# A speech joint network on one core: the first convolution of batch 0 by direct taps and two triple tiles instead of pair filtering

## The chip, the cores and the metric

The kernel runs on 1 core of one Trainium2 chip. The metric is the device time of one execution in microseconds (us). Five engines of the core work side by side, each with its own queue of instructions: PE (TensorE) multiplies matrices, DVE (VectorE), ACT (ScalarE) and POOL (GpSimd) work on elements, and SP (SyncE) issues the transfers (DMAs). Matrix products are written to PSUM, eight banks of 512 fp32 columns.

## The reference

x is 2 x 4000 x 512 (bf16). Two convolutions over time of five taps and stride 2 (computed as stride 1 and then halved), each followed by GELU, reduce 4000 steps to 2000 (h) and then 1000 (f); a joint network then adds each of 1000 steps to each of 8 label vectors, takes tanh, and multiplies by w_o.

```
xp = pad(x, 2)                                   # B, T, D = 2, 4000, 512; K = 5
h = gelu(sum(xp[:, i:i+T] @ w1[i] for i in range(5)))[:, ::2]
hp = pad(h, 2)
f = gelu(sum(hp[:, i:i+2000] @ w2[i] for i in range(5)))[:, ::2]
j = tanh((f @ w_f)[:, :, None] + (g @ w_g)[:, None])      # 2, 1000, 8, 512
out = j @ w_o                                             # 2, 1000, 8, 512
```

## The kernel before, in words

Everything is held with the 512 channels on partitions: four blocks k of 128 input channels, four blocks m of 128 output channels. A product of one weight slice with one operand is four matmuls (one for each k) into one PSUM bank (`mm`, L471).

**Three ways to compute the first convolution.**
- Direct (`direct`, L835): one product for each tap, 5 products of n columns for n outputs.
- Pair filtering (`Tile_`, L673): 7 products for 2n outputs, with filtered inputs (`xf`, `shift`) and filtered weights (`w1sums`, `w1sum13`). `c1`, `c2` and `c3` are its stages; between them ACT copies a bank out, and DVE adds it to another.
- Triples (`Triple` and `Unit`, L714 and L763): 9 products for 3n outputs. Operands are made by DVE and ACT (`step`): "planes" are three copies scaled by 2 on ACT, with a subtraction on DVE each; then nine sums on DVE (t2, tm, sm, t1, s1, t0, s0, ti, si) and two shifted copies on ACT (prev, next). Weights come from `w1part`. A Unit is one m of a tile, with stages `s1` to `s5`: t2; tm and sm; t1 and s1; t0 and s0; ti and si. Behind `s1` and `s2` ACT copies the bank out, behind `s3` DVE makes two posts (a SCALAR_TENSOR_TENSOR and a TENSOR_TENSOR), and three outputs go through ACT as GELU.

Batch 0's 2000 outputs are three tiles before: 504 outputs (blocks m = 0, 1 direct, m = 2, 3 pair-filtered), 504 pair-filtered, and `trip[0]` of 332 triples. `trip[1]` and `trip[2]` are batch 1 with 334 triples each, `trip[3]` and `trip[4]` the second convolution of both batches. Then comes the joint stage.

**Loads** (all on SP, in written order). `load_xr` brings two blocks of 128 x 4 rows of x untransposed; PE transposes them (L560), ACT and DVE copy them from PSUM to `xs`. Then the five taps of w1 in the order 0, 2, 4, 1, 3 (`load_w1`, L518; from the second on each waits until the load three places earlier has landed). Then transposing DMAs: four of 256 rows for `xs` (`load_x`), six of 336 rows for `xp[1]`, the operand of `trip[0]` (`load_x6`, L508), one small `xe` of the last 16 rows, of which POOL copies a column into `xp[1]` (`load_end`, L529), and six for batch 1. The rest (`load_rest`, `load_late`) is issued by slot in the loop over units.

**Order of the work.** `Plan` is a planner in the kernel itself. Each operation has an engine, what it reads and writes, and an estimated cost. `schedule` (L160) runs a list schedule (`once`) up to `PASSES` times, between passes `learn` (L190) shifts due times and holds back operations where PE stops, and the best order is kept. From `pl.pin = False` (L849) on, PE, POOL and SP take the lowest index that is ready, ACT and DVE the earliest due time. Loads keep their written order. The loop at L995 writes the stages of the units and at fixed slots (`when`, `steps`) the making of later operands, loads and weights. The banks are one list of eight; a unit takes a bank A at `s1` and a bank B at `s3`, and gives them back after `s4` and `s5`.

PE first multiplies zeros (`warm_mm`, 7 and 1 more).

Of the kernel before, what the change touches and what calls it, by code (L numbers as in the profile page):

```python
# [68 lines left out]
class Plan:  # L69
# [4 lines left out]
    PASSES = 32  # L74
# [85 lines left out]
    def schedule(self, pred):  # L160
# [16 lines left out]
        hold, best = [0.0] * n, None  # L177
# [12 lines left out]
    def learn(self, pred, got, late, hold):  # L190
# [5 lines left out]
        t, found = 0.0, False  # L196
        for i in order["pe"]:
            if start[i] - t > 0.1 and start[i] > 6.0:
                j = i
                for _ in range(30):  # L200
                    done = [(end[q] + (self.HOP if w else 0.0), q) for q, w in pred[j].items()]
                    if not done:
                        break
                    q = max(done)[1]
                    if self.ops[q].dma:
                        break
                    e, p = place[q]
                    if e in ("act", "dve") and p and start[q] > ready[q] + 0.03:
                        b = order[e][p - 1]
                        if start[b] < ready[q] - 0.02 and first[b] > first[q]:  # L210
                            hold[b] = max(hold[b], ready[q] - 0.01)
                        late[q] -= 0.1
                        found = True
                    j = q
            t = end[i]
        return found
# [128 lines left out]
def bass_standalone__seq2seq_rnn_t_joint__speech_kernel(  # L345
# [25 lines left out]
    NA, NB = 252, 504  # L371
    NT3 = (T2 + 2) // 3
    NL = 332
# [6 lines left out]
    NWARM = 7  # L380
    TAPS = (0, 2, 4, 1, 3)

    with ExitStack() as es:
# [22 lines left out]
        xr = [Buf(nc, f"xr{i}", [4, NK, P], BF16, h_off + 16384 + i * 4096) for i in range(2)]  # L406
        assert hT[0].end <= h_off + 16384 and xr[1].end <= cur[0]
        c_off = cur[0]
        cs = [at(f"cs{i}", [NT], FP32) for i in range(2)]
        ty = [at(f"ty{i}", [2, 256], FP32) for i in range(3)]  # L410
        s_off = cur[0]
        ws = [at(f"ws{i}", [NK, P * (2 if i == 2 else 1)], FP32) for i in range(3)]
# [6 lines left out]
        w1_h = at("w1_h", [NK, D], BF16)  # L419
        xe = [at(f"xe{b}", [NK, 16], BF16) for b in range(B)]  # L420
        assert cur[0] <= 229368, cur[0]
        sd = [Buf(nc, f"sd{i}", [3, 336], FP32, o) for i, o in enumerate((c_off, c_off + 4096, s_off + 4096))]
        assert sd[1].end <= ty[2].end and sd[2].end <= ws[2].end
# [6 lines left out]
        row = [Buf(nc, f"row{b}", [6, NK, 336], BF16, xt_off + b * xt[0].bytes) for b in range(B)]  # L430
# [57 lines left out]
        for ph in (2, 3):  # L488
            memset(xs[0][ph, :, 15:16])
# [5 lines left out]
        def load_xr(rt):  # L495
            dst = xr[rt][:].map(lambda a: a.rearrange("p r k c -> p (r k c)"))
            src = x[0, 4 * P * rt:4 * P * (rt + 1), :].rearrange("(p r) c -> p (r c)", r=4)
            return pl.dma("sp", lambda e: e.dma_start(dst.ap, src), (), (dst,))

        def load_x(s, ph, lo, hi):  # L500

            b, half = s // 2, s % 2
            i0 = half * NB + lo - 16
            dst = xs[s % 3][ph, :, lo:hi]
            src = x[b, 4 * i0 + ph:4 * (i0 + hi - lo - 1) + ph + 1:4, :]
            pl.dma("sp", lambda e: e.dma_start_transpose(out=dst.ap, in_=src), (), (dst,), nbytes=(hi - lo) * 2 * D, rate=175e3)  # L506

        def load_x6(i, b, ph, j0, col):  # L508

            r0 = b * T + 6 * j0 + ph  # L510
            dst = xp[i][ph, :, col:col + 336]
            src = x.rearrange("b t d -> (b t) d")[r0:r0 + 6 * 335 + 1:6, :]
            pl.dma("sp", lambda e: e.dma_start_transpose(out=dst.ap, in_=src), (), (dst,), nbytes=336 * 2 * D, rate=175e3, slack=0.0 if i == 1 else 1.0)  # L513

        came = [load_xr(rt) for rt in range(2)]
# [7 lines left out]

        came.append(load_w1(TAPS[0]))
# [4 lines left out]
        def load_end(i, b):  # L529
            memset(xp[i][4:6, :, 336:340])  # L530
            memset(xp[i][0:4, :, 337:340])
            for ph in (4, 0, 2, 1, 3, 5):
                load_x6(i, b, ph, 330, 0)
            e16, d = xe[b][:], xp[i][0:4, :, 336:337]
            pl.dma("sp", lambda e: e.dma_start_transpose(out=e16.ap, in_=x[b, T - 16:T, :]), (), (e16,), nbytes=65536)
            v = xe[b][:, 12:16].map(lambda a: a.rearrange("p k (r o) -> p r k o", o=1))
            pl.op("pool", lambda e: e.tensor_copy(out=d.ap, in_=v.ap), (v,), (d,), 0.15)  # L537

        load_end(1, 0)
        for ph in (4, 0, 2, 1, 3, 5):  # L540
            load_x6(2, 1, ph, 0, 16)
# [9 lines left out]
        for pp in range(2):  # L551
            for rt in range(2):
                for r in range(2):
                    bk = 4 * rt + 2 * r if not pp else 2 * rt
                    lo = bk * 1024 + pp * r * 512
                    pv = View(psb[:, lo:lo + 512].rearrange("p (k c) -> p k c", k=NK), np.array([bk]), True)

                    def fn(e, rt=rt, pp=pp, r=r, pv=pv):
                        for k in range(NK):
                            ins = e.transpose(pv.ap[:, k, :], xr[rt].h[:, 2 * r + pp, k, :], ident.h[:, :])  # L560
                        return ins
                    pl.op("pe", fn, (xr[rt][:], ident[:]), (pv,), 0.22 if pp else 0.43)
                    if not pp and not rt and r:
                        warm_mm(NWARM, NWARM + 1)
                    o = xs[0][2 * r + pp, :, 16 + rt * P:16 + (rt + 1) * P]
                    if pp or r:
                        act(o, pv, ACT.Copy)
                    else:
                        pl.op("dve", lambda e, o=o, pv=pv: e.tensor_copy(out=o.ap, in_=pv.ap), (pv,), (o,), vec_cost(o, (pv,)))

        def shift(src, off, dst, c0, n, which):

            r, d, kind = {"a0": (2, -1, 0), "a3": (0, 1, 2), "b1": (3, -1, 3)}[which]
            act(dst[kind, :, c0:c0 + n], src[r, :, off + d:off + d + n], ACT.Copy)

        def xf(src, off, dst, c0, n, which, keep=False):


            ph = lambda r: src[r, :, off:off + n]
            o = lambda kind: dst[kind, :, c0:c0 + n]  # L580
            h = NT // 2
            if which == "a0" and keep:
                tt("dve", o(0), src[2, :, off - 1:off - 1 + n], ph(2), sub)
            elif which == "b3" and keep:
                tt("dve", dst[0, :, h:h + n], ph(3), ph(1), sub)
            elif which == "a2" and keep:
                tt("dve", dst[1, :, h:h + n], ph(2), ph(0), sub)
            elif which == "a0":
                tt("dve", o(0), o(0), ph(2), sub)
            elif which == "a3":  # L590
                tt("dve", o(2), o(2), ph(0), sub)
            elif which == "b1":
                tt("dve", o(3), o(3), ph(1), sub)
            elif which == "b3":
                tt("dve", ph(3), ph(3), ph(1), sub)
            elif which == "a1":
                tt("dve", o(1), ph(0), ph(2), add)
            elif which == "a2":
                tt("dve", ph(2), ph(2), ph(0), sub)

        def operand(src, off, dst, c0, n, which, k, keep=False):
            if keep and which in ("b3", "a2"):
                return dst[("b3", "a2").index(which), k, NT // 2:NT // 2 + n]
            if which in ("a0", "a1", "a3", "b1"):
                return dst[{"a0": 0, "a1": 1, "a3": 2, "b1": 3}[which], k, c0:c0 + n]
            r = {"b3": 3, "b2": 1, "a2": 2}[which]
            return src[r, k, off:off + n]
# [239 lines left out]
        for w in ("b1", "a3"):  # L847
            t0.shift(w)
# [436 lines left out]
```

## Time and profile before

| | us |
|---|---|
| median of 3 runs (256.37 to 257.28) | 256.41 |
| the profiled execution | 257.11 |
| its span, first to last instruction | 255.3 |
| idle PE in the span | 8.4 |
| first matmul of the direct taps / of the triple tile | 8.27 / 37.42 |

| stretch (us) | PE busy | DVE busy | ACT busy |
|---|---|---|---|
| 0.00 to 6.40 | 5.21 | 1.00 | 2.08 |
| 6.40 to 12.80 | 5.00 | 3.94 | 3.64 |
| 12.80 to 19.20 | 6.36 | 6.10 | 5.70 |
| 19.20 to 25.60 | 6.40 | 6.27 | 5.92 |
| 25.60 to 32.00 | 6.40 | 6.14 | 3.98 |
| 32.00 to 38.40 | 4.99 | 5.23 | 5.64 |
| 38.40 to 44.80 | 5.79 | 6.40 | 6.04 |
| 64 to 128 | 64.00 | 52.49 | 46.71 |
| 128 to 192 | 63.95 | 52.55 | 63.27 |

The profile is one execution. Times in it are microseconds from the span's start; busy time of an engine is the union of its instructions, and what lies between them is idle, put down to what ended it. A line number such as L475 is that of the helper that records the operation, so operations are told apart by their tiles: `acc<-xs,w_sb` is a matmul that writes PSUM from the weights `w_sb` and the operand `xs`. SPq is SP's queue while it issues a DMA.

### The profile page before, as it was taken

What the parts mean: (1) busy time and instruction counts of PE and PEld (TensorE: products, weight loads), DVE (VectorE), ACT (ScalarE), POOL (GpSimd) and SP (SyncE); (2) the same over time, 40 slices, a digit from 0 to 9 for tenths busy, and PEclk for the clock granted to TensorE, in tenths of its full rate; (3) what the DMA queues carried; (4) which work ended last, traced back from release to release, by engine and by line L of the source; (5) the groups of instructions that cost most, each with busy time, mean ns of one, the idle gap of its engine ahead of it and who ended that gap; (6) DMA issues with size and microseconds to landing.
All of it is one profiled execution on the core that took longest, in us unless ns stands there. A gap on an engine that the chain in (4) does not pass through costs nothing.

```text
span 255.3 us, 5286 instructions
## 1 busy us (share of the span) xinstructions
PE 246.9 (97%) x1922; PEld 185.3 (73%) x1928; DVE 209.2 (82%) x335; ACT 214.2 (84%) x352; POOL 102.7 (40%) x107
## 2 busy tenths in 40 slices
PE   8799979999999999999999999999999999999994
PEld 4689965666666666667557878877778877787882
DVE  1699989994999998197346889789899999999673
ACT  3589689959968857885499999999999999999862
POOL 1000000000000000000708899787796999998800
PEclk9999999999999999999999999999999999999999
DMA  6999999979100015000001322342235266545565
GB/s 243 295 197 193 143 167 186 155 157 357 48 0 3 0 47 202 1 1 3 0 0 52 115 85 83 110 140 83 87 124 174 74 195 205 174 149 187 174 198 185
DMA packets 54631, 31.88 MB, mean 125 GB/s; under 512 B 31518, under 2 KB 54350, under 8 KB 54606
## 3 DMA queue, kind: packets, MB, share of 16 engines
q1 hardware_dynamic: 54318, 31.36, 46.2%
q8 instruction: 15, 0.25, 0.4%
q10 hardware_dynamic: 288, 0.20, 0.2%
q14 instruction: 10, 0.08, 0.1%
HBM read 7.86 MB, written 16.38 MB: 95 GB/s over the span
## 4 chain that ended last, share of the span: by engine, by line
PE 82%; SPq 7%; DMA 5%; ACT 2%; issue 1%; DVE 0%; POOL 0%
PE acc L475 82%; SPq L513 4%; SPq L506 3%; DMA w_sb<-in_w_dram 2%; DMA xe<-in_x_dram 2%; DMA xr<-in_x_dram 1%; ACT row L467 1%; ACT xp L467 0%; ACT sd L467 0%; DVE xp L462 0%; ACT w_x L467 0%; ACT hT L467 0%; POOL xp L537 0%; ACT ost L467 0%; SPq L493 0%
## 5 line engine op out<-in xcount | busy, mean ns | idle before, releaser
L462 DVE TENSOR_TENSOR og<-acc,sn 128x512 bf16<-128x512 f32 x84 | 55.5, 682 | 9.7 <-PE acc L475 7.2
L467 ACT ACTIVATE jT<-feT,geT 128x1000 bf16<-128x1000 f32 (+6 forms) x56 | 52.6, 1025 | 0.5 <-DVE feT L904 0.4
L475 PE MATMUL acc<-tw,ss 128*128 128x256 f16 x336 | 46.3, 273 | 0.0
L1027 ACT ACTIVATE sn<-acc 128x512 f32<-128x512 f32 x55 | 36.5, 675 | 2.6 <-PE acc L475 1.7
L475 PEld LDWEIGHTS acc<-tw,ss 128*128 128x128 f16 x336 | 32.5, 98 | 7.7 <-ACT sn L1027 0.2
L475 PE MATMUL acc<-row,w_sb 128*128 128x334 bf16 (+1 forms) x192 | 35.0, 305 | 0.0
L1090 POOL TENSOR_TENSOR ss<-jT 128x512 f16<-128x512 bf16 x24 | 29.1, 1225 | 12.5 <-ACT jT L467 10.4
L475 PE MATMUL acc<-wo_sb,jT 128*128 128x256 bf16 (+1 forms) x187 | 31.5, 292 | 0.3
L467 ACT ACTIVATE jX<-feT,geT 128x1000 bf16<-128x1000 f32 (+4 forms) x28 | 26.9, 1028 | 0.0
L475 PEld LDWEIGHTS acc<-row,w_sb 128*128 128x128 bf16 x192 | 18.4, 97 | 8.3 <-DVE acc L637 0.2
L475 PEld LDWEIGHTS acc<-wo_sb,jT 128*128 128x128 bf16 x192 | 18.7, 98 | 6.1
L467 ACT ACTIVATE hT<-acc 128x334 bf16<-128x334 f32 (+2 forms) x32 | 15.1, 483 | 8.3 <-PE acc L475 8.3
L459 POOL MEMSET hT<- 128x8 bf16 (+2 forms) x6 | 0.7, 148 | 51.2 <-ACT hT L467 46.6
L637 DVE SCALAR_TENSOR_TENSOR acc<-acc,sd 128x334 f32<-128x334 f32 (+1 forms) x20 | 10.1, 507 | 13.6 <-PE acc L475 13.4
L1028 DVE COPY sn<-acc 128x512 f32<-128x512 f32 x29 | 19.7, 682 | 1.3 <-PE acc L475 1.0
L467 ACT ACTIVATE sd<-acc 128x334 f32<-128x334 f32 (+1 forms) x40 | 17.4, 450 | 3.0 <-PE acc L475 2.6
L1090 POOL TENSOR_TENSOR ss<-jT,ss 128x512 f16<-128x512 bf16 x16 | 18.8, 1176 | 1.1 <-DVE ss L1090 0.7
L475 PE MATMUL acc<-xp,w_x 128*128 128x334 bf16 (+1 forms) x96 | 16.7, 304 | 1.4 <-DVE xp L462 1.4
L475 PE MATMUL acc<-hT,w_t 128*128 128x334 bf16 x96 | 17.6, 305 | 0.0
L475 PE MATMUL acc<-xp,w_sb 128*128 128x334 bf16 (+1 forms) x96 | 17.5, 304 | 0.0
L475 PE MATMUL acc<-wo_sb,ss 128*128 128x256 bf16 x112 | 17.0, 273 | 0.0
L462 DVE TENSOR_TENSOR row<-row 128x1336 bf16<-128x1336 bf16 (+1 forms) x20 | 16.7, 843 | 0.0
(110 smaller groups left out, 529.7 us busy)
## 6 DMA issues: line engine op xcount, KB each, us to landing
out_dram<-og SPq DMA_DIRECT2D x98, 128.0 KB, 2.0
w_sb<-in_w_dram SPq DMA_DIRECT2D x10, 512.0 KB, 5.5
out_dram<-ost SPq DMA_DIRECT2D x10, 128.0 KB, 2.0
xr<-in_x_dram SPq DMA_DIRECT2D x2, 512.0 KB, 3.6
wf_sb<-in_w_f_dram SPq DMA_DIRECT2D x1, 512.0 KB, 3.8
wg_sb<-in_w_g_dram SPq DMA_DIRECT2D x1, 512.0 KB, 4.8
wo_sb<-in_w_o_dram SPq DMA_DIRECT2D x1, 512.0 KB, 5.6
xp<-in_x_dram SPq DMA_TRANSPOSE x18, 4.8
```

The lines of the kernel that those rows point to most:

```text
L459: pl.op("pool", lambda e: e.memset(v.ap, 0.0), (), (v,))
L462: pl.op(eng, lambda e: e.tensor_tensor(out=o.ap, in0=a.ap, in1=b.ap, op=op), (a, b), (o,), 0.02 + 2.14e-3 * o.ap.free_size() if eng == "po ...
L467: pl.op("act", lambda e: e.activation(o.ap, i.ap, func, scale=scale, bias=0.0 if bias is None else bias.ap), rd, (o,), o.ap.free_size() * ...
L475: ins = e.matmul(o.ap, lhsT=l.ap, rhs=r.ap, start=start and n == 0, stop=stop and n == len(pairs) - 1, skip_group_check=not check)
L506: pl.dma("sp", lambda e: e.dma_start_transpose(out=dst.ap, in_=src), (), (dst,), nbytes=(hi - lo) * 2 * D, rate=175e3)
L513: pl.dma("sp", lambda e: e.dma_start_transpose(out=dst.ap, in_=src), (), (dst,), nbytes=336 * 2 * D, rate=175e3, slack=0.0 if i == 1 else 1.0)
L637: pl.op(eng, lambda e: e.scalar_tensor_tensor(out=o.ap, in0=a.ap, scalar=f, in1=b.ap, op0=ALU.mult, op1=add), (a, b), (o,), vec_cost(o, (a ...
L1027: pl.flex({"act": (lambda e: e.activation(o.ap, v.ap, ACT.Copy), 0.05 + n * 0.833e-3), "dve": (lambda e: e.tensor_copy(out=o.ap, in_=v.ap) ...
L1028: "dve": (lambda e: e.tensor_copy(out=o.ap, in_=v.ap), 0.065 + n * 1.04e-3)}, (v,), (o,))
L1090: fn = lambda e, o=S[i], x=x, y=y, op=op: e.tensor_tensor(out=o.ap, in0=x.ap, in1=y.ap, op=op)
```

## The change

- The untransposed loads are four blocks, of 128, 128, 128 and 64 partitions with two rows each (`XR`); PE transposes them into `eo`, even and odd rows apart, which lies where w2 comes later. ACT copies the even rows, DVE the odd ones.
- 444 outputs are computed directly, all four m, tap by tap into banks 0, 2, 4 and 6. `Tile_`, `xf`, `shift`, `w1sums` and what belongs to them are gone.
- `trip` has one more tile in front: `trip[0]` of NF = 184 triples from the new buffer `xa` (six transposing loads of 192 rows), `trip[1]` of NL = 336 triples from `xp[1]`. In `xa` the operand sm has a plane of its own. There are six tiles and 24 units, and the slots of what follows move by four.
- `xe` of batch 0 and its column copy are gone; POOL clears columns of `xp[1]` instead, two of them after the planes 4 and 5 have landed.
- The loads of `xa` stand between those of w1: after the third tap planes 4 and 0, after the fourth tap plane 2, after the fifth planes 1, 3 and 5. Then come those of `xp[1]`.
- `w1part` makes all of the triples' weights, the doubled tap 1 included (before, `w1twice` doubled it in place).
- Two bank lists, even (A) and odd (B), until the joint stage.
- The planner makes up to 100 passes, starts each from the best so far, and cycles through several steps and places. Five warm-up matmuls instead of eight.

```diff
-    PASSES = 32
+    PASSES = 100
...
-        for _ in range(self.PASSES):
-            got = self.once(pred, succ, late, hold)
-            if best is None or got[0] < best[0] - 1e-9:
-                best = got
-            if not self.learn(pred, got, late, hold):
+        for _ in range(self.PASSES):
+            new = list(late), list(hold)
+            if not self.learn(pred, best, *new, tried):
                 break
+            got = self.once(pred, succ, *new)
+            if got[0] < best[0] + 1e-9:
+                tried = tried + 1 if got[0] > best[0] - 1e-9 else 0
+                best, (late, hold) = got, new
+            else:
+                tried += 1
...
+    ND, NF = 444, 184
+    NL = 2 * NT3 - ND // 3 - NF
...
-    NWARM = 7
+    NWARM = 5
...
+    XR = [P] * ((ND + 1) // P) + [32 * -(-((ND + 1) % P) // 32)]
...
+        eo = Buf(nc, "eo", [2, NK, EW], BF16, w2_sb.end - w2_sb.bytes)
+        xa = Buf(nc, "xa", [7, NK, 224], BF16, xs[0].end - xs[0].bytes)
...
         came.append(load_w1(TAPS[0]))
-        for i in TAPS[1:]:
+        for i in TAPS[1:3]:
             came.append(load_w1(i, came[-3]))
-        for ph in (2, 3, 1, 0):
-            load_x(0, ph, 272, 528)
...
+        load_a(4, 0)
+        came.append(load_w1(TAPS[3], came[-3]))
+        load_a(2)
+        came.append(load_w1(TAPS[4], came[-3]))
+        load_a(1, 3, 5)
...
+        for ph in (4, 0, 2, 1, 3, 5):
+            load_x6(xp[1], 0, ph, JL, 0, slack=0.3)
+            if ph > 3:
+                memset(xp[1][ph, :, 335:336])
...
-        load_end(1, 0)
...
         def w1part(m):
...
             stt("dve", u, w(4), 4.0, w(0))
             stt("dve", u, w(2), 2.0, u)
             act(w1_x[1, :, sl], u, ACT.Copy, scale=1.0 / 3.0)
+            tt("dve", t, w(0), w(4), add)
+            tt("dve", v, t, w(2), sub)
+            act(w1_x[0, :, sl], v, ACT.Copy, scale=1.0 / 3.0)
+            tt("dve", w1_t[2, :, sl], t, w(2), add)
             tt("dve", w1_x[2, :, sl], w(1), w(3), sub)
+            tt("dve", w1_t[1, :, sl], w(1), w(3), add)
+            act(w1_t[0, :, sl], w(1), ACT.Copy, scale=2.0)
...
         def direct(i):
-            for m in (0, 1):
-                for s in range(2):
-                    r, d = tap_at[i][s]
-                    mm(ps.cols((4 + 2 * m) * NT + NA * s, NA),
-                       [(w1_sb[i, k, m * P:(m + 1) * P], xs[0][r, k, 16 + d:16 + d + NA]) for k in range(NK)],
-                       i == TAPS[0] and s == 0, i == TAPS[-1], False)
+            for m in range(NK):
+                mm(ps.cols(2 * m * NT, ND),
+                   [(w1_sb[i, k, m * P:(m + 1) * P], eo[i % 2, k, 15 + i // 2:15 + i // 2 + ND]) for k in range(NK)],
+                   i == TAPS[0], i == TAPS[-1], False)
...
-        for w in ("planes",) + STEPS[2:]:
+        for w in ("planes", "t2", "tm", "sm", "t1", "s1", "prev", "next", "t0", "s0", "ti", "si"):
             trip[0].step(w)
...
+        when(0, lambda: trip[1].step("planes"))
+        for i in range(1, 4):
+            steps(i, 1, (0, 2, 4, 8)[i], (1, 4, 8, 13)[i])
...
-        nu = 17
+        nu = 21
```

More of the change, by code (lines that the diff above doesn't have):

```diff
@@ L188, in schedule, with learn @@
         return order
-    def learn(self, pred, got, late, hold):
+    def learn(self, pred, got, late, hold, tried):
         _, order, start, end, ready, _ = got
         place = {i: (e, p) for e, o in order.items() for p, i in enumerate(o)}
-        first = list(late)
[L196 to L216, printed above, removed]
+        gaps, t = [], 0.0
+        for i in order["pe"]:
+            if start[i] - t > 0.05 and start[i] > 6.0:
+                gaps.append(i)
+            t = end[i]
+        if not gaps:
+            return False
+        kind, which = divmod(tried, len(gaps) + 1)
+        step, wait = ((0.1, True), (0.5, False), (0.0, True), (2.0, True), (0.3, False), (1.0, True))[kind % 6]
+        first = list(late)
+        for i in gaps if which == len(gaps) else gaps[which:which + 1]:
+            j = i
+            for _ in range(30):
+                done = [(end[q] + (self.HOP if w else 0.0), q) for q, w in pred[j].items()]
+                if not done:
+                    break
+                q = max(done)[1]
+                if self.ops[q].dma:
+                    break
+                e, p = place[q]
+                if e in ("act", "dve") and p and start[q] > ready[q] + 0.03:
+                    b = order[e][p - 1]
+                    if wait and start[b] < ready[q] - 0.02 and first[b] > first[q]:
+                        hold[b] = max(hold[b], ready[q] - 0.01)
+                    late[q] -= step
+                j = q
+        return True
     def once(self, pred, succ, late, hold):
@@ L550, in bass_standalone__seq2seq_rnn_t_joint__speech_kernel @@
         psb = ps.h[:, :].bitcast(BF16)
[L551 to L569, printed above, removed]
@@ L601, in operand @@
[L601 to L607, printed above, removed]
-        def weight(which, k, m):
-            sl = slice(m * P, (m + 1) * P)
-            taps = {"a0": 0, "b1": 1, "b3": 3, "a3": 4}
-            if which in taps:
-                return w1_sb[taps[which], k, sl]
-            return w1_h[k, sl] if which == "a1" else w1_t[{"a2": 0, "b2": 1}[which], k, sl]
@@ L755, in product @@
                 w, p = self.w[which]
-                n = NT3 if start else self.n
+                n = self.n
                 mm(ps.cols(bank * NT, n),
@@ L779, in s1 @@
             def s1(self):
-                self.A = banks.pop(0)
+                self.A = even.pop(0)
                 self.t.product("t2", self.m, self.A, True)
@@ L800, in s4 @@
                 self.t.out(0, self.m, self.pa())
-                banks.append(self.A)
+                even.append(self.A)
             def s5(self):
@@ L885, in bank @@
         def bank():
-            banks.append(banks.pop(0))
-            return banks[-1] * NT
+            even.append(even.pop(0))
+            return even[-1] * NT
         def ge():
@@ L1016, in sem_of @@
             return sems[key]
-        free = banks
+        even += odd
+        odd = free = even
         H = NT // 2
```

269 lines of the change are left out of this document (84 added, 185 removed).

## The prediction

> **What bounds the kernel now.** I read the page first: the busy line, the slices, the chain by engine.
>
> ```profile
> PE 246.9 (97%) x1922; PEld 185.3 (73%) x1928; DVE 209.2 (82%) x335; ACT 214.2 (84%) x352; POOL 102.7 (40%) x107
> ...
> PE   8799979999999999999999999999999999999994
> ...
> DVE  1699989994999998197346889789899999999673
> ...
> PE 82%; SPq 7%; DMA 5%; ACT 2%; issue 1%; DVE 0%; POOL 0%
> ```
>
> PE (TensorE) is busy 246.9 of 255.3 us: 8.4 us are idle, and the slices put them at the front and in the last slice. So the change can gain only in the first 60 us, by less PE time or by fewer stops. The waits of PE, and then the chain in order of time, say what the stops are:
>
> ```profile
> PE acc L475 <- DVE xp L462: 1.4, 1, 1.4
> PE acc L475 <- DMA w_sb<-in_w_dram: 1.4, 1, 1.4
> PE acc L475 <- DVE zero L482: 1.2, 1, 1.2
> PE acc L475 <- ACT sd L467: 0.6, 1, 0.6
> ```
>
> ```profile
> 28.45 4.81 DMA xe<-in_x_dram
> ...
> 33.31 0.45 POOL xp L537
> ...
> 33.79 1.33 ACT row L467
> ```
>
> 1.4 + 1.4 + 1.2 + 0.6 = 4.6 us; the other 3.7 are the tail, which the change leaves alone. The 1.2 us (zero tile) stay too. The stop of 1.4 us on `xp` is the start of the triple tile: 28 us of loads queue on SP up to the small `xe` load, then POOL, ACT and DVE follow it. The timelines of PE and of DVE (start, length, what) give durations; landings of loads are the issue rows of the trace, start plus time to landing.
>
> ```profile
> 5.43 1.44 PE L560 MATMUL acc<-ident,xr 128*128 128x128 bf16 x12
> 8.27 1.03 PE L475 MATMUL acc<-xs,w_sb 128*128 128x252 bf16 x8 [1.40 <-DMA w_sb<-in_w_dram]
> 9.13 0.61 PE L560 MATMUL acc<-ident,xr 128*128 128x128 bf16 x8
> 9.58 1.46 PE L475 MATMUL acc<-xs,w_sb 128*128 128x252 bf16 x12
> ...
> 37.42 2.45 PE L475 MATMUL acc<-xp,w_x 128*128 128x334 bf16 x16 [1.41 <-DVE xp L462]
> ```
>
> ```profile
> 10.82 0.69 DVE L462 TENSOR_TENSOR ws<-w_sb 128x512 f32<-128x512 bf16 x1 [1.79 <-DMA w_sb<-in_w_dram]
> ...
> 33.55 0.43 DVE L462 TENSOR_TENSOR w_x<-w_sb 128x512 bf16<-128x512 bf16 x1
> 35.14 0.86 DVE L462 TENSOR_TENSOR row<-row,xp 128x1336 bf16<-128x1336 bf16 x1 [1.16 <-ACT row L467]
> ```
>
> A matmul's step is the distance between starts. Eight of 252 columns take 9.13 - 8.27 = 0.86, so 107.5 ns; eight of 128 columns take 9.58 - 9.13 = 0.45, so 56 ns. Both are columns / 2.4 + 2.5 ns; the triples' 332 columns step by 141 ns in the same timeline. DVE works without a gap worth the name from 10.82 to 34 us. It is the second bound of this stretch, close behind PE.
>
> **PE, before and after.** Before: 248 matmuls of 252 columns x 107.5 = 26.7; 12 late transposes x 56 = 0.7; the triple tile 144 x 141 = 20.3. From 8.27 that is 55.9, and with stops of 1.4, 0.3 (18.3 to 18.6) and 0.6 the triple tile ends at about 58.3 us. After: direct 4 m x 5 taps x 4 k = 80 matmuls of 444 columns at 187.5 = 15.0; tile F (184 triples) 144 at 79.2 = 11.4; tile L (336) 144 at 142.5 = 20.5. Sum 46.9 against 47.7 before: PE time gains 0.8, all else must come from stops.
>
> A step of 79 ns for 184 columns is read between the rows of 128 (56 ns) and 252 (107.5), and the 16 matmuls of 16 columns at 120.64 take 0.55 us in all, so no weight load holds a step up there. The Trainium skill, TensorE: Matmul & The Clock Gate, section Back-to-back issue gap, says otherwise: for streams of weight load and matmul about 81 ns at 128 columns and 131 at 512. By that, as an estimate, 184 columns step by 88 ns and F is 12.7 us instead of 11.4; our 56 ns at 128 columns, each with its own weight load, speaks against it.
>
> **Start of direct.** Loads before the first tap: 896 KB of rows instead of 1 MB. The two 512 KB loads of before landed at 3.93 and 5.18, 1.25 us apart; quarters of that size land at about 3.3, 3.9, 4.6, 4.9. Two warm-up matmuls fewer (5 end at 3.3) leave PE no gap before the first rows. The 32 transposes then run at the early 107 ns (1.44 us for 12 above), some 3 us, and end near 6.5, copies at 7.3. The first weight (8.03 before) comes after 0.1 MB less: 7.7. Direct runs 7.7 to 22.7; its banks (0, 2, 4, 6) are free. Later taps are wanted 3 us apart and landed 1.4 to 2.1 apart before, so they are covered, even with three short transposes queued in front.
>
> **Loads on SP.** Before, a 344 KB transpose landed every 1.75 us (22.27 to 29.47, four steps), one of 262 KB every 1.5. 192 KB should take 1.1. After the third weight at 10.5: two transposes 12.7, weight 14.2, transpose 15.3, weight 16.9, three transposes 20.2, then L's six, 22 to 31. The fourth and fifth weight now wait on SP for the first and second (7.7, some 9.2), with every later transpose queued behind them; SP reaches them at about 8 and 10, after the transposes, so the wait is short. Before, `xp` came at 22.3 to 33.0 and `xe` at 33.3. Removed: `xe` with its SP issue of 1.2 us and the POOL copy (0.4), so nothing of L waits for 33.3 any more. Added: POOL clears one column of planes 4 and 5 after their landing (0.12 us for 32 elements at 27.39); behind it on POOL stand only other clears, and plane 4, landed at 22, is wanted at 33. Batch 1's loads follow as before, some 2 us sooner, and have 20 us in hand.
>
> **DVE, the sum that I take to decide.** Steps from the DVE timeline: 512 f32 0.60, STT 0.61 to 0.72, 512 bf16 0.33, 1008 bf16 0.60, 1328 bf16 0.77; 744 elements then take 0.455. Work from the third tap's landing (10.8 before, 10.5 after: the sums need taps 0 and 4) to L's first operand t2:
> - gone: 9 filter sums x 0.60 = 5.4 (three more lay ahead of 10.8), 6 pair posts x 0.34 = 2.0, 4 scalings x 0.21 = 0.8, and some 15 us of weight sums that come back in another form;
> - weights: per m two STT 1.33, three f32 1.8, two bf16 0.66 = 3.8, x 4 = 15.2. The four doublings of `w1_sb[1]` go from ACT in L to ACT in `w1part`;
> - F's operands: 3 planes + 9 sums = 12 x 0.455 = 5.5; F's posts: 4 x (0.40 + 0.27) = 2.7;
> - L: one plane and t2, 2 x 0.77 = 1.5.
> Sum 24.9, from 10.5: 35.4; with 0.8 us of dependent pairs and waits (before, DVE lost 1.5 on the same way, 1.2 of them to `xe`) 36.2. Before it was 37.3. So the cover for what was removed is not there: DVE has as much to do as before, only the wait for `xe` falls away. PE without stops would end F at 7.7 + 15.0 + 11.4 = 34.1, so PE stops for some 2 us in F and at L's start: F's third and fourth unit (t2 wanted at 25.9 and 28.7) wait for `w1part` of m = 2 and 3, of which DVE has done two by 22.7 (12.2 us of work, 5 of it F's operands).
>
> **ACT**: weights 12 x 0.52, four GELUs 2.0, F's copies 5 x 0.72, F's evictions 20 x 0.27, L's copies 3 x 1.22: 21 us of the 28 from 8 to 36. It hides, if its order is good; before, its order cost the 0.57 at 41.2, and I keep 0.4 for that.
>
> **Rest.** L's 8 posts and 10 sums and the next tile's operands are as before (DVE was done with them at 58.4 and then idle for 3.4 us), shifted by as much as L. Two bank pools of four instead of one of eight cost nothing: a unit holds its banks for under three units. The further passes of the planner can gain only where PE stops: after 41.78 it stops for some 0.3 us in all before the tail; a worse order there costs at most some tenths.
>
> **Sum.** L starts at 36.2, 0.4 stop, 20.5: 57.1 against 58.3. That is 1.2 us less span: 254.1 instead of 255.3, and with the 1.8 around the span 255.9 for the profiled execution (257.11). The median of the runs shown, 256.41, is 0.7 below that execution; I apply the difference to it: 255.2.
>
> **Rivals.**
> 1. Stops nearly vanish: DVE's order puts weights first and L's first operands land in slack. 7.7 + 46.9 + 0.4 = 55.0, 3.3 less: 253.1. For it: loads come earlier and ACT is freer; against it: the DVE sum. With DVE half-way there 254.2. Chance 0.2. By the skill's step (above) its best would be 254.4.
> 2. Nothing gained: DVE or ACT order loses what `xe` gave, or the PE clock starts late. Before, PE took 5.4 us of work (1.2 to 6.6) at 107 ns per 128 columns and was fast at 9.13, after a gap of 1.4 us. Fewer warm-ups and waits between four row loads may leave direct at half speed for up to 5.4 us: 2.7 lost, F ends at 36.8, L at 58.1. Range 255.8 to 257.5. Chance 0.2.
> 3. Slower: the twelve transposes keep the queue longer than their size says. An issue took up to 2.86 us beside weights (the second `xs` load). L's t2 needs the ninth (six of F, three of L), from 10.5 with 3.1 us of weights between. At 2.15 us each it lands at 33 and begins to hold L; from 2.5 us each L starts after 38.7 and the run is over 0.5% slower; at 2.86 each L starts at 42.3, 6.1 later than forecast: 261. Against it: 1.1 to 1.75 per transpose in the rows. Chance 0.1.
> The forecast, 254.6 to 255.8, has 0.5.
>
> **Chances.** A measurement of this kernel tells about 0.5% (1.3 us) from no change, so 255.1 and 257.7 are the bounds. Half of the forecast and all of rival 1 lie below 255.1, with a little of rival 2: faster 0.48. Same 0.42, slower 0.10. The range leaves out the best of rival 1 and all of rival 3: 253.4 to 257.0.
>
> **What would show it.** Right: 184-column matmuls 79 ns apart; direct from 7.7 at 187 ns; L's first matmul near 36 after a wait for DVE; DVE full from 10.5 to 57; no `xe` ahead of L. Wrong: PE waits for DMA in F (rival 3), 370 ns steps in direct (rival 2), L before 35 (rival 1), or new PE stops after 60 us, which no step here prices.

## The result, and the profile after

Slower by about half a per cent: 258.57 us (median of 22 runs, 256.19 to 260.61) beside 256.76 for the kernel before on the same chips; ratio 1.0054, interval 1.0028 to 1.0079. Two later series of the unaltered changed kernel gave 1.0028 (1.0000 to 1.0055) and 1.0044 (1.0016 to 1.0072); over all three its median is 257.9 (46 runs). A ratio leaves out runs that lie more than 1.5% above the fastest of the same kernel. The profiled execution took 257.44 us, with a span of 255.6 (before: 257.11 and 255.3), so it is one of the faster ones and shows only 0.3 us of the loss.

The page after, the same rows ("..." marks lines left out, here and below):

```profile
PE 248.5 (97%) x1901; PEld 180.0 (70%) x1901; DVE 207.0 (81%) x338; ACT 211.9 (83%) x356; POOL 102.6 (40%) x107
...
PE   6999989999999999999999999999999999999994
...
DVE  1299999981999999198346889789899999989673
...
PE 81%; DVE 8%; DMA 4%; SPq 4%; issue 1%; ACT 0%; DVEq 0%
```

The chain now has 8% DVE where it had none, and 4% SPq where it had 7%: the loads are still on it up to 21 us, and behind them it runs through DVE to 44 us. F is the tile of 184 triples and L the tile of 336, as in the prediction. The timelines of PE and DVE:

```profile
6.25 1.55 PE L581 MATMUL acc<-ident,xr 128*128 128x128 bf16 x16 [0.80 <-DMA xr<-in_x_dram]
8.07 16.29 PE L487 MATMUL acc<-eo,w_sb 128*128 128x444 bf16 x80 [0.26 <-ACT eo L479]
24.20 1.12 PE L487 MATMUL acc<-xa,w_x 128*128 128x184 bf16 x12
...
34.10 0.49 PE L487 MATMUL acc<-xa,w_x 128*128 128x184 bf16 x4 [0.68 <-DVE w_x L474]
```

```profile
11.73 0.69 DVE L591 SCALAR_TENSOR_TENSOR wu<-w_sb 128x512 f32<-128x512 bf16 x1 [3.59 <-DMA w_sb<-in_w_dram]
...
21.21 1.01 DVE L474 TENSOR_TENSOR xa<-xa 128x736 bf16<-128x736 bf16 x2 [0.30 <-DMA xa<-in_x_dram]
...
27.96 0.36 DVE L591 SCALAR_TENSOR_TENSOR acc<-acc,sd 128x184 f32<-128x184 f32 x1
```

The direct taps take 16.29 us for 80 matmuls; at 187.5 ns they would take 15.0 and the drain of the last one. The first six stepped by 370 ns: the granted clock turned full at 10.28 (6.70 before). That is 1.1 us. F starts at 24.2 and has its last matmul at 43.3, woven into L. From F's start to 44.2 PE stands for 2.9 us in small stops (the distances between starts, less columns / 2.4 + 2.5 ns). DVE begins at 11.73, when the third tap lands, and waits once more before 44 us, for a plane of F that lands at 21.19. The end of F and L together follows as a sum: 8.07 + 46.92 + 1.13 + 2.92 = 59.04, and for the kernel before 8.27 + 47.63 + 2.90 = 58.80.

The first matmul of the second convolution (operand `hT`) is a good mark for what the first 60 us cost, for both kernels do the same work from there on. The kernel before, then the changed one:

```profile
95.09 0.73 PE L475 MATMUL acc<-hT,w_t 128*128 128x334 bf16 x4
...
95.37 0.73 PE L487 MATMUL acc<-hT,w_t 128*128 128x334 bf16 x4
```

### The profile page after: what moved, and what is told of

The parts are those of the page before. It is cut to its first block, busy times and chain, and to the rows that moved or that the text cites. A ratio compares the mean times of both kernels' runs of the same rounds, so it can differ in the third digit from the quotient of the medians.

```text
span 255.6 us, 5244 instructions
## 1 busy us (share of the span) xinstructions
PE 248.5 (97%) x1901; PEld 180.0 (70%) x1901; DVE 207.0 (81%) x338; ACT 211.9 (83%) x356; POOL 102.6 (40%) x107
## 4 chain that ended last, share of the span: by engine, by line
PE 81%; DVE 8%; DMA 4%; SPq 4%; issue 1%; ACT 0%; DVEq 0%
PE acc L487 81%; SPq L518 3%; DMA xa<-in_x_dram 2%; DVE row L474 2%; DMA xr<-in_x_dram 2%; DVE xp L474 1%; DVE w_t L474 1%; DVE xa L474 1%; DVE wu L591 1%; SPq L505 1%; DVE ssum L474 1%; SPq L511 0%; DVE ws L474 0%; DVE acc L591 0%; DVE sd L474 0%
## 5 line engine op out<-in xcount | busy, mean ns | idle before, releaser
L487 PE MATMUL acc<-row,w_sb 128*128 128x334 bf16 (+2 forms) x224 | 38.9, 296 | 0.1
L487 PE MATMUL acc<-wo_sb,jT 128*128 128x256 bf16 (+1 forms) x192 | 32.1, 295 | 0.0
L487 PEld LDWEIGHTS acc<-row,w_sb 128*128 128x128 bf16 x224 | 20.9, 97 | 9.2 <-DVE acc L591 0.6
L591 DVE SCALAR_TENSOR_TENSOR acc<-acc,sd 128x334 f32<-128x334 f32 (+2 forms) x24 | 11.6, 482 | 15.6 <-PE acc L487 15.6
L479 ACT ACTIVATE sd<-acc 128x334 f32<-128x334 f32 (+2 forms) x48 | 19.9, 433 | 4.5 <-PE acc L487 3.3
L479 ACT ACTIVATE hT<-acc 128x334 bf16<-128x334 f32 (+3 forms) x36 | 15.2, 436 | 9.1 <-PE acc L487 8.8
L474 DVE TENSOR_TENSOR row<-row 128x1336 bf16<-128x1336 bf16 (+2 forms) x24 | 19.0, 793 | 0.0
L487 PE MATMUL acc<-xp,w_t 128*128 128x334 bf16 (+1 forms) x96 | 17.4, 305 | 0.0
L487 PE MATMUL acc<-xp,w_x 128*128 128x334 bf16 (+1 forms) x96 | 16.9, 305 | 0.0
```

The lines of the kernel that those rows point to most:

```text
L474: pl.op(eng, lambda e: e.tensor_tensor(out=o.ap, in0=a.ap, in1=b.ap, op=op), (a, b), (o,), 0.02 + 2.14e-3 * o.ap.free_size() if eng == "po ...
L479: pl.op("act", lambda e: e.activation(o.ap, i.ap, func, scale=scale, bias=0.0 if bias is None else bias.ap), rd, (o,), o.ap.free_size() * ...
L487: ins = e.matmul(o.ap, lhsT=l.ap, rhs=r.ap, start=start and n == 0, stop=stop and n == len(pairs) - 1, skip_group_check=not check)
L591: pl.op(eng, lambda e: e.scalar_tensor_tensor(out=o.ap, in0=a.ap, scalar=f, in1=b.ap, op0=ALU.mult, op1=add), (a, b), (o,), vec_cost(o, (a ...
```

## The experiments

Two theories. **DVE**: the stretch ends when DVE's queue, full from the third tap on, is worked off. **Clock**: PE has gaps before the direct taps, the full clock comes late, and that is lost at the end. "Own order" means that every queue has the order of the kernel named; "planned anew" means that the planner made another. All ratios are to the kernel before, which ran beside them; of most edits only the lines that matter are shown.

**The changed kernel unaltered**, twice.

> The changed kernel unaltered, beside the others on one chip. DVE theory (the conv1 stretch ends when a DVE queue, full from the third tap's landing at 11.7 us, is worked off, so PE's late clock is hidden): the ratio to before is again about 1.005, and in this second profile DVE is full from the third tap's landing to about 44 us. Clock theory (PE has too little to do before the direct taps, the granted clock turns full late, and each lost microsecond of the direct taps comes out at the end): the same ratio, and the total of this profile follows the moment at which the step of the 444-column matmuls falls from 370 to 187 ns (10.28 us in the first profile).

> The changed kernel unaltered, once more, beside these two: ratio 1.002 to 1.006. Another profile of it: the third tap's landing, the moment of full clock, PE's stops up to 44 us, and whether it has a long stop in the joint stage.

Measured: 1.0028 and 1.0044. In both profiles the clock was full from about 5, at half for one stretch of 3.41 us (from 8.14 and 8.65), and full again: 1.7 us lost. F's start and end move together: 24.20 to 43.32 in the profile of the result, 24.50 to 43.64 in the first of these, 24.63 to 43.76 in the second. The first has a span of 255.7; the second has 257.6, by a stop elsewhere:

```profile
PE acc L487 <- DVE og L474: 1.7, 1, 1.7
```

That one ends at 218 us, in the joint stage, which the change does not touch. The prediction named stops of PE after 60 us as a sign of being wrong, and priced none.

**More warm-ups**, planned anew (`NWARM` 6, two after the second block, one after the last).

> Four more warm-up matmuls, in the gaps between the row transposes and ahead of the direct taps, so that PE has work from 1.2 to 8 us. Clock theory: full clock before the direct taps begin, 1.1 us or more off the time, ratio to before 0.995 to 1.001. DVE theory: the direct taps end 1.1 us earlier, but the triple tile waits that much longer for DVE; time as the unaltered kernel within 0.3 us, ratio about 1.004.

Measured: 1.0118 (1.0083 to 1.0153). Clock full at 5.3, and the direct taps lost nothing, but PE lost 6.2 us between F's start and 44 us: some 1.6 of them because the clock was at half again from 25.75 to 29.16, behind two stops of PE of 1.1 us each, the rest in stops. So the run does not test the clock before the direct taps; it shows that the planner's order is a term of its own. Most of the next runs therefore keep the order.

**The same warm-ups, own order** (three instead of four, `NWARM` stays 5).

```diff
                         ins = e.transpose(...)
+                    for _ in range({1: 2, 3: 1}.get(rt, 0) if r else 0):
+                        e.matmul(ps.h[:, NT:2 * NT], lhsT=zero.h[:, 0:P], rhs=zero.h[:, :], start=True, stop=True)
```

> As the run with more warm-ups, but every engine keeps the changed kernel's own order: two extra matmuls of zeros behind the second block's transposes and one behind the last, no new plan. Clock theory: full clock before the direct taps, time 1.1 us or more under the changed kernel, ratio to before 0.998 or less (changed kernel: 1.0054 and 1.0028). DVE theory: the direct taps end at about 23.1 instead of 24.2, PE's stops between 24 and 44 us grow by the same 1.1, ratio 1.003 to 1.005.

Measured: 1.0044 (1.0011 to 1.0077), span 255.0. The timelines of PE and DVE:

```profile
7.54 15.22 PE L487 MATMUL acc<-eo,w_sb 128*128 128x444 bf16 x80 [0.70 <-ACT eo L479]
```

```profile
11.82 0.69 DVE L593 SCALAR_TENSOR_TENSOR wu<-w_sb 128x512 f32<-128x512 bf16 x1 [4.97 <-DMA w_sb<-in_w_dram]
```

The clock is full in time, F starts 1.6 us earlier (22.6), and its last matmul comes 0.3 earlier (43.0): the stops grew from 2.9 to 4.2. Most of the growth is one stop of 0.9 us up to 24.33, where F's third block waits for a GELU on ACT, which in ACT's own order stands behind a scaling that waits for DVE until 23.2. DVE has no wait between 11.82 and its first post for F. So here DVE's queue is the bound, and the clock theory alone falls: its ratio of 0.998 or less did not come, nor the end 1.1 us earlier.

**Less DVE work**, planned anew and in own order.

```diff
-            tt("dve", w1_x[2, :, sl], w(1), w(3), sub)
-            tt("dve", w1_t[1, :, sl], w(1), w(3), add)
```

> Leaves out the sum and the difference of taps 1 and 3 in all four blocks (8 DVE operations of 0.33 us, 2.6 us in all; the products s1 and sm use taps 1 and 3 themselves, so h of batch 0 and 1 is another). DVE theory: PE's stops between 24 and 44 us shrink by most of 2.6 us, time 1.5 to 2.5 us lower than the unaltered kernel. Clock theory: the loss at half clock stays, and the time falls by less than 0.7 us.

> As the run with fewer DVE sums, but every engine keeps the changed kernel's own order: the eight operations stay in the queue with 32 elements each (about 0.27 us less each, 2.1 us in all), and the products s1 and sm use taps 1 and 3 themselves, so that the first convolution's values are others. DVE theory: the dense part of PE begins about 2 us earlier than 44.2, ratio to before 0.995 to 0.998. Clock theory: PE's stops shrink by little, ratio 1.002 to 1.005.

Measured: 1.0020 (0.9994 to 1.0047) and, in own order, 0.9995 (0.9968 to 1.0021). Beside the changed kernel's 1.0028 to 1.0054 that is 0.2 to 0.9 us and 0.8 to 1.5 us less, under what the DVE theory expected of either. In own order the stops fell from 2.9 to 2.0, although the clock came late there (1.5 us lost).

**When the taps land.** First, without SP's waits ahead of the second and third tap (planned anew); then all taps ahead of F's transposing loads (own order).

> The second and third tap no longer wait on SP for the third and fourth row block to land; they are issued right behind the first tap. DVE theory: the third tap lands about 1 us earlier than 11.7 and the whole DVE queue and the end with it, 0.7 to 1 us off the time. Clock theory: nothing unless the first tap's landing moves the start of the direct taps; time within 0.4 us of the unaltered kernel.

> All five taps ahead of the six transposing loads of the 184-triple tile, on SP; every other queue keeps the changed kernel's order. DVE theory: the third tap lands at about 10.8 instead of 11.7 (as in the kernel before), the DVE queue and the end come 0.7 to 0.9 us earlier, unless the planes of that tile, now some 2 us later, hold DVE instead; ratio 0.999 to 1.002. Clock theory: no effect but through the first tap's landing; ratio 1.003 to 1.005.

Measured: taps 1.0004 (0.9965 to 1.0043) over the four runs counted; the other eight took 259.98 to 261.34 us. In the profile, one of these eight, the three taps were issued at 2.7, 3.4 and 3.9, and the first landed at 10.1 instead of 7.8, the third at 12.95; the clock was full at 14.0. Late: 1.0135 (1.0098 to 1.0171); the third tap came at 11.8 all the same, the first three planes of F 2.5 to 3.6 us later. Both expectations failed: without the waits the third tap lands no earlier, and the transposes do not hold it. What is left is the row blocks, with whose last landing (6.7) the third tap is issued. Hence the next run: two loads of 512 KB as before.

```diff
-        came = [load_xr(rt) for rt in range(NX)]
+            src = x[0, 512 * i:512 * (i + 1), :].rearrange("(p r) c -> p (r c)", r=4)
+        came = [load_two(i) for i in range(2)]
```

> The changed kernel with its own order on every other queue, but the rows of x come as in the kernel before, in two loads of 512 KB with 4 KB a partition instead of four loads with 2 KB (rows enter the transposes in another order, so the first 444 outputs are others). If the four small loads are what holds the taps back, the rows are there at about 5.2 instead of 6.7, the third tap at 10.8 instead of 11.7, and by the DVE theory the end comes 0.6 to 0.9 us earlier; ratio 0.999 to 1.002. If the small loads are not the cause, the third tap lands at 11.5 or later again.

Measured: 1.0004 (0.9974 to 1.0035), span 254.5, with the second convolution from 94.47 on: no loss is left in this profile, and none that the interval shows. The interval still takes in the changed kernel's 1.0028, and a run below with such loads is at 1.0044, so the profile says more here than the ratio. Timelines of PE and DVE, then SP's issues of the row loads, four in the changed kernel and two in the kernel before:

```profile
4.12 3.13 PE L586 MATMUL acc<-ident,xr 128*128 128x128 bf16 x32 [0.61 <-DMA xrr<-in_x_dram]
8.24 15.21 PE L487 MATMUL acc<-eo,w_sb 128*128 128x444 bf16 x80 [0.99 <-ACT eo L479]
```

```profile
10.90 0.69 DVE L596 SCALAR_TENSOR_TENSOR wu<-w_sb 128x512 f32<-128x512 bf16 x1 [3.32 <-DMA w_sb<-in_w_dram]
```

```profile
0.73 1.97 SPq L511 DMA_DIRECT2D xr<-in_x_dram  x4
...
0.74 0.87 SPq L498 DMA_DIRECT2D xr<-in_x_dram  x2
```

The rows are there at 5.27 instead of 6.71, the 32 transposes run in one piece, the clock is full at 6.95, the third tap lands at 10.88, and F runs from 23.3 to 42.4. Part of the later landing is SP's issuing: the last of four is issued at 2.12, the second of two at 1.19, so of the 1.5 us between 6.71 and the 5.18 of the kernel before 0.9 are that.

**Taps in the order 0, 4, 2, 1, 3** (`TAPS`), alone, with the warm-ups, with the eight sums on POOL as well, and together with two row loads (of 128 and 96 partitions, 4 KB each) and one more matmul of zeros behind the last transposes; the last in own order and planned anew. DVE's first sums need taps 0 and 4.

> The changed kernel with its own order on every queue, but the taps loaded and multiplied in the order 0, 4, 2, 1, 3 instead of 0, 2, 4, 1, 3. The first sums on DVE need taps 0 and 4, so its queue can begin with the second landing (10.1) instead of the third (11.7); two operations (1.2 us) fit in between. DVE theory: everything behind comes up to 1.2 us earlier, as far as PE's direct taps allow; ratio to before 0.998 to 1.002 (changed kernel: 1.0054 and 1.0028). Clock theory: no change.

> The same with three extra matmuls of zeros between the row transposes. Both bounds of the stretch are eased at once (DVE begins 1.2 us earlier, PE's direct taps end about 1.1 us earlier): if PE and DVE bound it together, the time falls by about 1.1 us where each alone gives a third of that; ratio 0.994 to 0.999. If DVE alone bounds it, as the run without the extra matmuls.

> Taps in the order 0, 4, 2, 1, 3, the three extra matmuls, and the eight sums and differences of taps 1 and 3 on POOL instead of DVE (1.2 us each there, done by about 28); all else in the changed kernel's own order. DVE theory: DVE has 2.6 us less to do and begins 1.2 us earlier, PE's stops between 24 and 44 us fall under 1.5 us; ratio 0.990 to 0.995, faster than both kernels. If POOL slows DVE down while both work, the gain is less than that of the run with the sums left out.

> The changed kernel with its own order on the engines, its rows loaded in two loads with 4 KB a partition (128 and 96 partitions, four rows each; the copies out of PSUM write every second column) and the taps in the order 0, 4, 2, 1, 3. Both remedies that each moved DVE's beginning (to 10.9 and to 10.4) at once. DVE theory: DVE begins at about 9.5, two operations ahead of the third tap at 10.8; time 1 to 2 us under the changed kernel and under both single remedies (ratios 1.0004 and 1.0025); ratio 0.994 to 0.999. If PE's direct taps bound the stretch by then, no better than the two 4 KB loads alone, 1.000.

> The same, but planned anew by the kernel's own planner. If an order made for the later third tap costs something, the new one is 0.3 us or more faster than the same kernel with the old order; if the planner's order is a matter of luck, it is off by as much either way. Ratio 0.992 to 1.003.

Measured: 1.0025 (0.9992 to 1.0057), 0.9997 (0.9965 to 1.0029), 1.0185 (1.0143 to 1.0227), 1.0044 (1.0012 to 1.0075) and 1.0007 (0.9978 to 1.0037). None of the five is clearly faster than the kernel before, and only the last lies in the range expected for it; the profile of the fourth bears out its second alternative, PE as the bound. In the profile with the warm-ups the third tap landed at 13.2 instead of 11.7, so the two bounds were not eased at once there. On POOL the sums take what they spare: DVE's sums of 736 bf16 elements, 0.46 us apart otherwise, go in step with POOL's (timelines of POOL and DVE):

```profile
19.03 1.45 POOL L474 TENSOR_TENSOR w_t<-w_sb 128x512 bf16<-128x512 bf16 x1
```

```profile
19.40 2.90 DVE L474 TENSOR_TENSOR row<-row 128x736 bf16<-128x736 bf16 x2
```

In that profile the clock was at half from 25.90 to 32.73 as well.

With both remedies (taps and row loads) DVE begins at 9.0 instead of 10.9, but F starts at 23.28 and ends at 42.41, exactly as with the row loads alone. So DVE's beginning is not the bound by then. The table puts the profiles in own order side by side (us; F from its first to the start of its last matmul; stops from F's start to 44.2; the first post is DVE's first on F; the last column is the first matmul of the second convolution, 95.09 in the kernel before):

| | DVE begins | F | PE's stops | first post | second conv. |
|---|---|---|---|---|---|
| changed | 11.73 | 24.20 to 43.32 | 2.9 | 27.96 | 95.37 |
| changed, again | 11.61 | 24.50 to 43.64 | 2.9 | 28.28 | 95.69 |
| warm-ups | 11.82 | 22.60 to 43.01 | 4.2 | 27.66 | 95.05 |
| row loads | 10.90 | 23.29 to 42.42 | 2.9 | 27.06 | 94.47 |
| taps | 10.39 | 22.95 to 42.41 | 3.3 | 27.06 | 94.46 |
| taps and warm-ups | 11.74 | 23.81 to 43.43 | 3.4 | 28.07 | 95.47 |
| row loads and taps | 9.02 | 23.28 to 42.41 | 2.9 | 27.05 | 94.46 |
| all taps first | 11.84 | 24.29 to 45.25 | 4.5 | 29.90 | 97.30 |

The last matmul of F comes 15.3 to 15.4 us after the first post in all of them, for behind it DVE is full to 44 us, and PE waits for what stands there. So what matters is when DVE makes that post, and three things can hold it. The first is PE: where DVE waits for the post, it comes 3.8 us after F's start. So it is with the row loads, in the changed kernel, again, and with row loads and taps:

```profile
27.05 0.36 DVE L593 SCALAR_TENSOR_TENSOR acc<-acc,sd 128x184 f32<-128x184 f32 x1 [0.34 <-PE acc L487]
```

The second is DVE's own queue: with the warm-ups the post comes 15.8 us after DVE's beginning, without a wait between. The third was in neither theory, the planes of F: with the taps reordered alone, DVE waits for the fifth of them, and the post comes 6.75 us after that wait, as in the changed kernel (21.21 and 27.96). With all taps first the planes came later still, and with taps and warm-ups the chain runs through the fifth tap, which landed at 19.60. The wait with the taps reordered alone:

```profile
20.31 1.01 DVE L474 TENSOR_TENSOR xa<-xa 128x736 bf16<-128x736 bf16 x2 [0.38 <-DMA xa<-in_x_dram]
```

In the changed kernel's first profile the three meet within 0.4 us: 24.20 + 3.77 = 27.97 by PE, 11.73 + 15.84 = 27.57 by DVE's queue, 21.21 + 6.75 = 27.96 by the planes. In its two later profiles, which lost 1.7 us to the clock, PE is the bound. DVE's queue stands right behind it: the end of F with the warm-ups, 43.01, is only 0.3 to 0.8 us earlier than in these three profiles.

**The planner.** Here the kernel before has only the changed planner: 100 passes, each started from the best plan so far.

```diff
-    PASSES = 32
+    PASSES = 100
...
-            if not self.learn(pred, got, late, hold):
+            if not self.learn(pred, best, *new, tried):
```

> The kernel before with nothing but the changed planner (up to 100 passes from the best so far). The changed kernel's own plan hardly depends on the planner (with the old one, PE, ACT, POOL and SP have the same order, and DVE differs in two places), so both theories say that the planner is no cause of the loss there. Here it moves 18 places on PE, 43 on ACT and 65 on DVE: faster by up to 0.6 us if the stops of 0.57 and 1.41 us can be planned away, ratio 0.997 to 1.001.

Measured: 1.0022 (0.9989 to 1.0056). No gain, and no difference from 1 that the interval shows.

**The kernel before with the taps reordered**, own order.

> The kernel before with its own order on every queue and nothing changed but the order of the taps, 0, 4, 2, 1, 3. Its first DVE sums need taps 0 and 4 as well. DVE theory: DVE begins 1.4 us earlier (9.4 instead of 10.8), but in this kernel the triple tile also waits for the last small load (33.3 us) and its POOL copy, so the end comes at most 0.3 us earlier; ratio 0.998 to 1.000. If DVE alone bounds it, 0.995.

Measured: 0.9998 (0.9970 to 1.0025); PE's stop of 1.4 us at `xp` is unchanged. That agrees with the chain of the kernel before, where the small load `xe` holds that start.

**The joint stage.** In the profile of the run with both remedies one DVE sum waits behind POOL's, and PE behind DVE (timeline):

```profile
211.33 4.18 DVE L966 TENSOR_TENSOR ss<-jT,ss 128x512 f16<-128x512 bf16 x1
...
211.85 2.28 POOL L966 TENSOR_TENSOR ss<-jT 128x512 f16<-128x512 bf16 x2
...
216.77 0.61 PE L487 MATMUL acc<-tw,jT 128*128 128x256 f16 x4 [1.73 <-DVE og L474]
```

The last two runs clear the tile instead of POOL's sums, in both kernels.

> The changed kernel with its own order on every queue; in the joint stage the operand sums that the plan gives to POOL are replaced by clearing their tile there (the output is another), so that POOL no longer reads beside DVE, while DVE's own sums stay. If collisions of POOL and DVE in the joint stage (one DVE sum took 4.18 us and PE stood for 1.7 us in one profile) are what makes the changed kernel's runs slower and far apart, the runs lie within 2 us of each other, the time is 1 us or more lower than the changed kernel's, and the loss against the kernel before treated alike is gone. If the loss sits in the first 44 us, this run and the same treatment of the kernel before differ by 0.5 to 1.5 us still.

> The kernel before with its own order on every queue and the same replacement of POOL's sums. Collision theory: as fast as the changed kernel so treated, within 0.4 us, runs closer together. DVE theory: 0.5 to 1.5 us faster than the changed kernel so treated.

Measured: 257.55 us (256.45 to 257.67, ratio 1.0016, 0.9991 to 1.0041) and 256.59 (255.34 to 257.95, ratio 0.9987, 0.9957 to 1.0016). The changed kernel's runs close up, from 256.2 to 260.6 in its first series to 1.2 us; of its 46 unaltered runs 16 took over 258.5 us (12 of them in the first series of 22), of these twelve none. So DVE's collisions with POOL (a DVE sum that waits for POOL's, and PE for DVE) spread them. Its median stays 1.0 us over the other's: that part of the loss does not hang on the collisions. About half of it goes with the clock. Six of its twelve runs, and two of the other's, had a mean granted clock of 0.991 or 0.993 (one stretch of 3.41 us at half clock in 255 us gives 0.993); among the runs at 0.997 and more the medians are 257.0 and 256.6. Why the collisions come in more runs of one variant than of another stays open, and it hides differences of a few tenths of a per cent between all versions here.

## Why the prediction was wrong

The forecast was 255.2 us (253.4 to 257.0), a gain of 1.2; measured was 258.57, a loss. Of the 3.4 us between them 1.5 lie in the profiled execution, 257.44 where the prediction had 255.9. The other 1.8 lie in the last line of its sum, which took the median to be 0.7 below the profiled execution, as in three runs of the kernel before; here it was 1.1 above. Step by step:

- **PE's sum** held: steps of 79 ns at 184 columns (0.48 us for four with the drain, groups 0.32 apart), 187 at 444. The Trainium skill, TensorE: Matmul & The Clock Gate, section Back-to-back issue gap, would have F at 88 ns, as an estimate between its two figures; the trace decides for 79.
- **Start of direct** failed, and with it most of the time. "Quarters of that size land at about 3.3, 3.9, 4.6, 4.9": they landed at 3.5, 4.2, 6.1, 6.7. The step left out that SP issues them one after the other, the last at 2.12. "The first weight 7.7" was 7.8, but PE had a gap of 0.8 us among the transposes, the clock came at 10.28, and F started at 24.2 instead of 22.7. The clock was named as rival 2 and priced at up to 2.7; it was 1.1 to 1.7.
- **Loads**: the third tap at 11.7 instead of 10.5, by the same term: SP issues it when the last row block has landed, 6.7 instead of 4.9. The fourth and fifth came at 15.3 and 18.2 instead of 14.2 and 16.9, and the transposes of F and L within 2.5 us of the forecast. L did not wait for its transposes, which was rival 3; but DVE waited 0.3 us for a plane of F, which no step priced.
- **The DVE sum** was right in what it showed (DVE has as much to do as before), and L's t2 was done at 35.1 instead of 36.2. But it was read as a sum up to L's start, with F done by then. F was not: DVE's order serves both tiles and puts L's t2 ahead of the last weights of F and of three of its eight posts. PE waited for weights at 34.1 and 36.8, F's matmuls alternate with L's until 43.3, and PE stood for 2.9 us instead of 2.5.
- Together 1.5 (F's start) and 0.4 (stops) against a forecast gain of 1.2, and 0.5 that the kernel before ends later than reckoned (58.8, not 58.3): 0.2 us slower; the two spans say 0.3. Those are two single profiles: the second convolution begins at 95.4 to 95.9 in four profiles of the changed kernel (one of them with the cleared tiles), at 94.3 to 95.1 in three of the kernel before (one with the cleared tiles, one with the taps reordered).
- The rest up to 1.0 us between the medians is shown by the runs that clear the tiles to be outside the collisions. In the three series 22 of 46 runs of the changed kernel had a granted clock under 0.995 over the span, 23 of 145 of the kernel before. In those 46 the clock does not tell long runs from short ones (medians 257.8 under 0.995 and 258.2 above); with the tiles cleared it does. The other 0.8 us of the first series' 1.8 go with its 12 runs above 258.5; that these are collisions is likely, but not shown.
- What `xe` cost was gained (no stop at L's start but 0.07 us), and spent by the row loads.
- Two slips in the prediction move nothing: the four steps from 22.27 to 29.47 are 1.80 us each, not 1.75, and rival 2's end of L, 58.1, is 0.4 more than its own terms give.

## What to carry to other kernels

Cutting a first load into more pieces is a change of its own: price when the last piece is issued and when it lands, and what is issued behind it, from rows of the same kind. Where two engines finish a stretch within half a microsecond of each other, mending one shows little; the row loads moved F's start and DVE's beginning at once, by 0.9 and 0.8 us, and the end of F by 0.9. Look then for the operation where the two meet, here the first post: the end came a fixed time after it. Hold the queues' order fixed in experiments where a planner would make another.

## What was not expected of the hardware

- Three loads of 256 KB and one of 128 KB, 2 KB a partition, landed last at 5.8 to 6.7 us; two of 512 KB, 4 KB a partition, at 5.2 to 5.4 (1 MB). With 4 KB a partition but 512 and 384 KB, the last landed at 5.5 and 5.9 in two profiles, so how much the bytes a partition matter beside the issue time is not shown.
- The granted clock went back to half for 3.41 us after it had been full (8.14 to 11.55 in one profile), with a gap of 1.5 us on PE before (6.33 to 7.78). The same program had its clock full for the first time at 4.7, 5.2 and 10.3 us. The Trainium skill, TensorE: Matmul & The Clock Gate, section Part 1: The HAM clock gate, tells of a free-running window of about 3.4 us; the trace agrees with its length.
- DVE sums with two inputs in SBUF go in step with POOL's: 1.45 us instead of 0.46 with bf16 results, 1.63 instead of 0.68 for one with an fp32 result (at 25.05 in the run with the eight sums on POOL). The Trainium skill, SBUF — State Buffer, section Who interferes with whom, names that pair of instructions as one that contends; the trace agrees.
